# A fixed, interleaved instruction order and DMA transposes in a fused attention and GLU kernel on one Trainium2 core

## The chip, the cores and the metric

The kernel runs on one core of a Trainium2 chip. The metric is the device time of one execution in microseconds (us). The kernel before takes 261.02 us (median of 16 runs, 260.28 to 262.19).

PE is TensorE, the matrix engine, and PEld are its weight loads. DVE is VectorE, ACT is ScalarE, POOL is GpSimd and SP is the engine whose queue issues nearly all of the DMAs. The "span" is the time from the first to the last event of the profiled execution; the measured time is about 1.8 us longer.

## The reference

```python
xn = layernorm(x)                       # x: 2048 x 512, bf16
# branch A: linear attention, 32 heads of 16
q, k, v = split(xn @ wqkv)
phi(t)  = concat(softmax(t @ w_phi), softmax(-(t @ w_phi)))     # per head
kv, z   = phi(k)^T v, sum(phi(k))
o       = (phi(q) kv) / (phi(q) z + 1e-6)
# branch B: bilinear GLU, F = 1792
h       = (xn @ w_gate) * (xn @ w_up)
out     = x + o @ wo + h @ w_down
```

The sequence is 16 tiles of 128 tokens, in 4 groups. Both branches need xn with the features on the partitions, so xn is transposed; so are o and, for the fold of w_phi into wk and wq, the two weights.

## The kernel before

Each token tile passes through `a1_tile` (keys and values). The groups of four tiles then pass through the query stage, and the GLU and the output sum (`fin`) stand last in the source. A scheduler orders the instructions of every engine; it starts GLU matmuls early where it finds room.

```python
def ln_group(ng):                       # layer norm of 4 tiles, then transposes on PE
    ...
    for c in range(DC):
        tp = ps_tr.tile([P, TT], BF16, name="tp")
        for ni in range(GT):
            nc.tensor.transpose(out=tp[:, ni * P:(ni + 1) * P],
                                in_=xn_tiles[ni][:, c * P:(c + 1) * P], identity=ident[:])
        nc.scalar.copy(out=xnT[:, c, ng * TT:(ng + 1) * TT], in_=tp[:])

def a1_tile(n):
    pk = xnT tile @ W1k                               # PE, 4 matmuls of 512 columns
    e  = exp(pk), exp(-pk)                            # ACT
    vp = xnT tile @ wv ; vt = copy(vp)                # PE, ACT
    sums, rs, phik = reduce, reciprocal, e * rs       # DVE
    kv += phik^T vt                                   # PE, 8 matmuls of 129 columns

# query stage, per tile: nd on PE, five DVE steps, o_tok on POOL, then
otp = ps_pq.tile([P, DC, P], BF16, name="pq")
for c in range(DC):
    nc.tensor.transpose(out=otp[:, c, :], in_=o_tok[:, c * P:(c + 1) * P], identity=ident[:])
nc.scalar.copy(out=oT[:, :, n * P:(n + 1) * P], in_=otp[:])

# GLU, per block f: g = xnT @ wg (4 matmuls), u = xnT @ wu (4), g_sb = copy(g) on ACT, hT = u * g_sb on DVE
# fin, per tile: 14 matmuls hT @ wd and 4 matmuls oT @ wo
```

(The lines of `a1_tile` and the comments are shortened.)

The softmax here doesn't subtract the row's maximum and nothing guards it: scores larger than these inputs give would overflow.

## Time and profile before

| | before |
|---|---|
| time, span | 261.02 us, 258.8 us |
| PE busy | 92% of the span |
| DVE, ACT busy | 57%, 40% |
| first matmul starts, last ends | 5.4 us, 255.1 us |
| PE work, counted at issue pace | 226.5 us |

From the page of the kernel before: busy time by engine, three of the lines of 40 slices (tenths busy, and for PEclk the granted clock in tenths), and the head of the chain of work that ended last.

```profile
PE 239.3 (92%) x1376; PEld 115.5 (45%) x1376; DVE 148.1 (57%) x263; ACT 104.0 (40%) x209; POOL 22.2 (9%) x41
...
PE   0599999999999999999989999989999999999994
...
DVE  4286999999939972880983785487211211233221
...
PEclk9999999999999999999999999999999999999999
...
PE 67%; DVE 17%; POOL 5%; DMA 3%; ACT 2%; issue 2%; SPq 1%; POOLq 1%; DVEq 0%; ACTq 0%
```

PE looks full from the third slice on, yet only 67% of the chain is PE. Matmuls overlap in the records: one is on record for 0.38 us, but the next starts after 0.216 us. A gap of up to 0.16 us between two starts therefore does not show as idle, and a longer one shows 0.16 us too short. The busy share of 92% is therefore no good measure of the gaps here. The remedy used is to count work at issue pace: the number of matmuls of each kind, times the distance between starts where they follow each other without a wait.

That distance can be read where many stand together. From the timeline of the kernel before (start, length, then engine, line, operation and count; in brackets the idle time before it and what ended it), first at the beginning, then in the query stage:

```profile
11.40 0.63 PE L152 MATMUL tp<-ident,xn 128*128 128x128 bf16 x4
11.82 0.63 PE L188 MATMUL vp<-wv,xnT 128*128 128x512 bf16 x1
12.25 0.63 PE L279 MATMUL g<-xnT,wg 128*128 128x512 bf16 x1
...
106.78 0.40 PE L269 MATMUL pq<-ident,o_tok 128*128 128x128 bf16 x4 [0.52 <-POOL o_tok L264]
107.02 0.81 PE L279 MATMUL g<-xnT,wg 128*128 128x512 bf16 x3
107.67 1.03 PE L284 MATMUL u<-xnT,wu 128*128 128x512 bf16 x4
108.53 0.59 PE L279 MATMUL g<-xnT,wg 128*128 128x512 bf16 x2
108.96 0.66 PE L247 MATMUL nd<-KVZ,E 128*128 128x144 bf16 x8
```

At 107.67 four matmuls take 0.86 us (108.53 less 107.67). Around 12 us a single matmul takes 0.43 us, twice the steady 0.216; from 14.31 us on the pace is the steady one. That the clock is still low around 12 us is read from this pace alone: the PEclk row reads 9 there as well. Until 8.96 us PE waits for the layer norm of the four tiles; then the work comes in single matmuls, one chunk of xnT at a time. By 16.0 us only 12 full-width matmuls have started. At 106.78 PE has waited 0.52 us for o_tok. The waits list of the kernel before (engine and line, waited for, total us, times, longest) has these:

```profile
PEld L269 <- POOL o_tok L264: 13.1, 16, 1.0
PEld L152 <- DVE xn L146: 10.7, 10, 5.4
PE tp L152 <- DVE xn L146: 8.1, 4, 5.4
...
PE pq L269 <- POOL o_tok L264: 5.4, 12, 0.5
```

In sum PE issues 226.5 us of work in the 249.7 us between its first and last matmul: some 23 us are gaps (time lost to the half pace at the start is counted among them).

### The profile page before, as it was taken

The page shows a single profiled execution, that of the slowest core. Times are in us where ns is not written, and L with a number is a line of the kernel's source. Part 1 is how long each engine was busy: PE and PEld are TensorE (multiplying, and loading weights), DVE is VectorE, ACT ScalarE, POOL GpSimd, SP SyncE. Part 2 cuts the span into 40 slices and gives each one's busy share as a digit, 9 for nine tenths or more (in the row PEclk, how much of TensorE's full clock was granted, in tenths as well). Part 3 has the DMA queues.
Part 4 walks back from the last instruction along what each step waited for, and adds up shares of the span by engine and source line. Part 5 has one row for each costly group of instructions (what it writes and reads, how often), then busy time and mean ns, then how long its engine had stood idle before and what let it go on. Part 6 is the DMA issues. An engine that isn't in the chain of part 4 may idle for free.

```text
span 258.8 us, 3516 instructions
## 1 busy us (share of the span) xinstructions
PE 239.3 (92%) x1376; PEld 115.5 (45%) x1376; DVE 148.1 (57%) x263; ACT 104.0 (40%) x209; POOL 22.2 (9%) x41
## 2 busy tenths in 40 slices
PE   0599999999999999999989999989999999999994
PEld 0255444555454554444444454444444444444441
DVE  4286999999939972880983785487211211233221
ACT  3459745776367457248336445624000000013000
POOL 5200000000000000131131113033000000000000
PEclk9999999999999999999999999999999999999999
DMA  6999600000000000000000000000001101100001
GB/s 188 364 389 349 214 1 4 0 0 3 0 0 0 3 0 0 3 1 0 3 1 0 0 3 0 0 3 0 11 31 43 35 26 41 37 27 0 20 20 41
DMA packets 11007, 12.02 MB, mean 46 GB/s; under 512 B 1008, under 2 KB 9968, under 8 KB 10992
## 3 DMA queue, kind: packets, MB, share of 16 engines
q1 hardware_dynamic: 10992, 11.81, 13.8%
q8 instruction: 10, 0.16, 0.3%
q14 instruction: 5, 0.04, 0.1%
HBM read 9.72 MB, written 2.10 MB: 46 GB/s over the span
## 4 chain that ended last, share of the span: by engine, by line
PE 67%; DVE 17%; POOL 5%; DMA 3%; ACT 2%; issue 2%; SPq 1%; POOLq 1%; DVEq 0%; ACTq 0%
PE fin L295 19%; PE u L284 14%; PE g L279 11%; PE pq L236 6%; POOL o_tok L264 5%; PE fin L298 5%; DVE sums L194 5%; DVE hT L290 4%; DVE phik L198 3%; DMA wg<-in_B_w_gate_dram 3%; PE vp L188 3%; PE pk L181 2%; PE pq L269 2%; PE tp L152 2%; PE kv L203 2%
## 5 line engine op out<-in xcount | busy, mean ns | idle before, releaser
L289 ACT CAST g_sb<-g 128x512 bf16<-128x512 f32 x56 | 32.9, 587 | 86.2 <-PE g L279 84.6
L279 PE MATMUL g<-xnT,wg 128*128 128x512 bf16 x224 | 63.5, 381 | 0.2
L284 PE MATMUL u<-xnT,wu 128*128 128x512 bf16 x224 | 62.0, 381 | 0.3 <-DVE hT L290 0.2
L290 DVE TENSOR_TENSOR hT<-u,g_sb 128x512 bf16<-128x512 f32 x56 | 38.4, 687 | 41.6 <-PE u L284 40.7
L295 PE MATMUL fin<-wd,hT 128*128 128x512 bf16 x224 | 51.0, 379 | 0.0
L301 DVE TENSOR_TENSOR o_sb<-fin,xall 128x512 bf16<-128x512 f32 x16 | 11.1, 692 | 51.0 <-PE fin L298 51.0
L295 PEld LDWEIGHTS <-hT 128*128 128x128 bf16 x224 | 21.9, 98 | 26.4
L284 PEld LDWEIGHTS <-wu 128*128 128x128 bf16 x224 | 21.0, 98 | 23.0 <-issue 3.7
L264 POOL TENSOR_TENSOR o_tok<-sm,rden 128x512 bf16<-128x512 f32 x16 | 16.9, 1056 | 155.2 <-PE u L284 134.0
L279 PEld LDWEIGHTS <-wg 128*128 128x128 bf16 x224 | 21.1, 98 | 19.1 <-DMA wg<-in_B_w_gate_dram 0.7
L194 DVE TENSOR_REDUCE sums<-e 128x64 f32<-128x1024 f32 x16 | 19.2, 1201 | 0.4 <-ACT e L185 0.4
L198 DVE TENSOR_TENSOR phik<-e,rs 128x1024 bf16<-128x1024 f32 x16 | 19.4, 1211 | 0.0
L188 PE MATMUL vp<-wv,xnT 128*128 128x512 bf16 x64 | 18.9, 389 | 0.0
L181 PE MATMUL pk<-W1k,xnT 128*128 128x512 bf16 x64 | 17.8, 377 | 0.5
L152 PE MATMUL tp<-ident,xn 128*128 128x128 bf16 x64 | 9.1, 240 | 8.8 <-DVE xn L146 8.1
L298 PE MATMUL fin<-wo,oT 128*128 128x512 bf16 x64 | 16.4, 379 | 0.0
L270 ACT COPY oT<-pq 128x512 bf16<-128x512 bf16 x16 | 9.4, 585 | 17.0 <-PE pq L269 16.5
L236 PE MATMUL pq<-xnT,W1q 128*128 128x512 bf16 x64 | 15.6, 378 | 0.0
L141 DVE BATCH_NORM_STATS2 stats<-xall 128x6 f32<-128x512 bf16 x16 | 10.5, 675 | 7.6 <-DMA xall<-in_A_x_dram 7.6
L184 ACT ACTIVATE e<-pk 128x512 f32<-128x512 f32 x16 | 9.6, 599 | 10.8 <-DVE phik L198 5.7
L152 PEld LDWEIGHTS <-xn 128*128 128x128 bf16 x64 | 5.7, 106 | 15.1 <-DVE xn L146 10.7
L154 ACT COPY xnT<-tp 128x512 bf16<-128x512 bf16 x16 | 9.4, 590 | 6.3 <-PE tp L152 6.1
(48 smaller groups left out, 204.8 us busy)
## 6 DMA issues: line engine op xcount, KB each, us to landing
out_dram<-o_sb SPq DMA_DIRECT2D x16, 128.0 KB, 1.7
wd<-in_B_w_down_dram SPq DMA_DIRECT2D x1, 1792.0 KB, 13.6
xall<-in_A_x_dram SPq DMA_DIRECT2D x3, 512.0 KB, 12.3
wg<-in_B_w_gate_dram SPq DMA_DIRECT2D x1, 1280.0 KB, 11.2
wu<-in_B_w_up_dram SPq DMA_DIRECT2D x1, 1280.0 KB, 12.6
wqk<-in_A_wqkv_dram SPq DMA_DIRECT2D x2, 512.0 KB, 7.8
wv<-in_A_wqkv_dram SPq DMA_DIRECT2D x1, 512.0 KB, 6.7
wg<-in_B_w_gate_dram SPq DMA_DIRECT2D x1, 512.0 KB, 7.6
```

Of the source, the lines that this page charges most:

```text
L181: nc.tensor.matmul(pk[:], lhsT=xnT[:, j, n * P:(n + 1) * P], rhs=W1k[:, j, :], start=(j == 0), stop=(j == DC - 1))
L188: nc.tensor.matmul(vp[:], lhsT=xnT[:, j, n * P:(n + 1) * P], rhs=wv[:, j, :], start=(j == 0), stop=(j == DC - 1))
L194: nc.vector.tensor_reduce(out=sums[:], in_=ev, axis=AX.X, op=ALU.add)
L198: nc.vector.tensor_tensor(out=phik[:].rearrange("p s (h f) -> p (s h) f", f=DH), in0=ev, in1=rs[:].to_broadcast((P, 2 * H, DH)), op=ALU.mult)
L236: nc.tensor.matmul(pq[:], lhsT=W1q[:, j, cq * P:(cq + 1) * P], rhs=xnT[:, j, T * TT:(T + 1) * TT], start=(j == 0), stop=(j == DC - 1))
L264: nc.gpsimd.tensor_tensor(out=o_tok[:].rearrange("p (a h d) -> p a h d", a=2, d=DH), in0=sm[:, :, :, 0:DH], in1=rden[:].to_broadcast((P, 2 ...
L279: nc.tensor.matmul(gps[:], lhsT=wg[:, c, f * P:(f + 1) * P], rhs=xnT[:, c, T * TT:(T + 1) * TT], start=(c == 0), stop=(c == DC - 1))
L284: nc.tensor.matmul(ups[:], lhsT=wu[:, c, f * P:(f + 1) * P], rhs=xnT[:, c, T * TT:(T + 1) * TT], start=(c == 0), stop=(c == DC - 1))
L289: nc.scalar.copy(out=g_sb[:], in_=gps[:])
L290: nc.vector.tensor_tensor(out=hT[:, f, :], in0=ups[:], in1=g_sb[:], op=ALU.mult)
L295: nc.tensor.matmul(fin[:], lhsT=hT[:, f, t4 * P:(t4 + 1) * P], rhs=wd[:, f, :], start=(f == 0), stop=False)
L298: nc.tensor.matmul(fin[:], lhsT=oT[:, c, n * P:(n + 1) * P], rhs=wo[:, c, :], start=False, stop=(c == DC - 1))
```

## The change

There are two ideas in one change. The first: the order of every engine is written by hand (`manual_schedule`). A GLU block (1.73 us of PE) stands after each step whose result has to come back from ACT or DVE, the kv matmuls of a tile come one pass late, and `fin` is interleaved with `nd`. The second: 144 of the 160 transposes leave PE. xn (tiles 4 to 15) and o_tok are stored to DRAM and read back by a transposing DMA; wk and wq are loaded by a transposing DMA. Twelve dummy matmuls on zeros are added at the start, meant to raise the clock before the real ones (without them the time was 1.6 us longer: e5 below).

```diff
+    ctx.enter_context(tc.manual_schedule())
-    oT = xpool.tile([P, DC, S], BF16, name="oT")
+    oT = xnT
+    nc.sync.dma_start_transpose(out=wkT[:], in_=A_wqkv[:, D:2 * D])
...
+    wps = ps_gu.tile([P, TT], F32, name="gu")
+    for i in range(10):
+        nc.tensor.matmul(wps[:], lhsT=warm[:, 0:P], rhs=warm[:], start=True, stop=True)
...
-            for c in range(DC):                       # transposes of xn on PE, copies on ACT
-                tp = ps_tr.tile([P, TT], BF16, name="tp")
-                ...
+            nc.sync.dma_start(out=xds[ng][(ni - 1) * P:(ni + 1) * P, :]..., in_=xns[ng][:, ni - 1:ni + 1, :])
+            if ni == GT - 1:
+                nc.sync.dma_start_transpose(out=xnT[:, :, ng * TT:(ng + 1) * TT], in_=xds[ng][:])
...
-        for n in range(NT):
-            if n % GT == 0 and n > 0:
-                ln_group(n // GT)
-            a1_tile(n)
+        for n in range(NT):                           # G() is one GLU block
+            RED(n)
+            G()
+            if n >= GT: VV(n)
+            if n > 0: KV(n - 1)
+            LNr, LNx, TRst for the tiles of a later group
+            RCP(n); PHI(n)
+            G()
+            LNs for the tiles of a later group
+            PK(n + 1); EX(n + 1)
+            G()
...
-                otp = ps_pq.tile([P, DC, P], BF16, name="pq")       # transposes of o_tok on PE
-                ...
+            nc.sync.dma_start(out=ods[T][t4 * P:(t4 + 1) * P, :], in_=o_tok[:])
+            ...
+                nc.sync.dma_start_transpose(out=oT[:, :, T * TT:(T + 1) * TT], in_=ods[T][:])
...
+        for n in range(NT):
+            ND(n)
+            Pq(T + 1, t4, ps_pq, "pq")
+            Fin(fin_next) if n > GT else G()
```

(Shortened in places; the bodies are those of the kernel before. The GLU, `fin` and the first transposes share one PSUM pool of three banks.)

## The prediction

> **What bounds it now.** 261.35 us, span 258.8. The page gives TensorE (PE) 92% busy, VectorE 57%, ScalarE 40%; the chain of waits is 67% PE. Busy hides gaps, because matmul records overlap, so I count issue pace from the timeline: a 512-column matmul every 0.216 us (fin x14 in 3.02), nd x8 0.50, kv x8 0.47, a 128-column transpose or fold 0.056. The groups list 928 512-column matmuls, 128 nd, 128 kv, 160 transposes (64 of xn, 32 of wqk, 64 of o_tok) and 32 fold matmuls: 200.2 + 8.0 + 7.5 + 9.0 + 1.8 = 226.5 us. PE runs from 5.4 to 255.2, 249.8 us, so about 23 us are gaps. About 6 of them lie before 16 us: until 14 us matmuls are 0.43 us apart (cold clock[...]) and wait for layer-norm tiles (waits list: weight loads on xn 10.7 us, matmuls 8.1 us). The rest are short waits on VectorE, ScalarE and o_tok, scattered by the automatic schedule. The tail after the last matmul is 3.7 us.
>
> **What the change does.** A hand-fixed order on every engine: GLU blocks (1.73 us of PE each) lie between the attention steps so that PE has work during each VectorE/ScalarE latency; fin is interleaved with nd. 144 of 160 transposes move to the DMA (xn of groups 1 to 3, wk, wq, o_tok): minus 8.1 us of PE and about 36 PSUM copies. Adds 12 dummy matmuls that warm the clock while PE waits anyway, about 28 DMA issues, and some 7 MB of DRAM traffic on a queue idle after 32 us.
>
> **Cost on the critical path.** PE work left: 226.5 - 8.1 = 218.4. About 6.1 us of it (16 transposes, fold, four vp, one pk) precede the steady loop, which I expect to start at 14 us: first xn at 5, transposed wk near 8 to 9. Then 212.3 us of PE. Per tile PE needs 7.5 us with vp, 6.5 without; VectorE (sums 1.20, phik 1.21, rs 0.54, three hT 2.06, layer norm 1.25) needs 6.3, so PE stays the limit except in tiles 0 to 2, where two layer norms fall in one tile: about 2 us lost. Change of stage and bank waits: 1.5 us. Tail 3.3 us. Span 233, plus 2.2 us by which the time exceeds the span: **235 us**, range **230 to 244**. Chances: faster by over 2% 0.96, within 2% 0.03, slower 0.01.
>
> **Signs.** Right: PE pace 0.86 per four matmuls nearly unbroken from 14 us to the end; gaps under 6 us after the loop starts; cold matmuls only before 6 us; 1,232 real matmuls. Wrong: pk or vp of tiles 4, 8, 12, or fin of tiles 0 and 12, waiting for the DMA to xnT.
>
> **What would break it.** No transposing DMA is in this trace. [...] The slack from layer norm to first use is about 8.5 us, less 2 for the store, and at the end about 5 us; if a transpose takes 8 us, each of four places loses 2 to 3 us (about 245). A late wk delays the start one for one. [...]

14 + 212.3 + 2 + 1.5 + 3.3 make the span of 233, and with 2.2 the 235 us. "Cold" here means the pace of 0.43 us a matmul; that the dummies warm the clock had no measurement yet (e5 below gives one).

## The result, and the profile after

| | before | after |
|---|---|---|
| time (median) | 261.02 us (16 runs) | 230.34 us (8 runs, 230.03 to 231.11) |
| span | 258.8 us | 228.6 us |
| PE busy | 92% | 98% |
| matmul records | 1,376 | 1,262 |
| first real matmul starts, last ends | 5.4, 255.1 us | 5.53, 225.85 us |

The ratio of the times is 0.8823 (95% interval 0.8805 to 0.8841). Ratios here are the mean time of one kernel's fast runs over that of the other's of the same rounds, so not quite the ratio of the medians.

The same parts of the page of the changed kernel:

```profile
PE 224.2 (98%) x1262; PEld 111.8 (49%) x1262; DVE 150.8 (66%) x261; ACT 86.1 (38%) x177; POOL 22.4 (10%) x42
...
PE   7999999999999999999999999999999999999995
...
DVE  4769998877977786676557447996555556762121
...
PEclk9999999999999999999999999999999999999999
...
PE 98%; ACT 0%; DVE 0%; issue 0%
```

The chain is now PE and nothing else. The timeline of PE in the changed kernel, at the start of the loop and around the only wait for another engine that its waits list has for a PE matmul of the loop or later:

```profile
12.77 1.03 PE L143 MATMUL gu<-xnT,wg 128*128 128x512 bf16 x4
13.63 1.03 PE L149 MATMUL gu<-xnT,wu 128*128 128x512 bf16 x4
14.49 1.03 PE L143 MATMUL gu<-xnT,wg 128*128 128x512 bf16 x4
...
132.14 1.02 PE L180 MATMUL vp<-xnT,W1q 128*128 128x512 bf16 x4 [0.31 <-ACT E L183]
```

Each group of four starts 0.86 us after the one before it. That is the pace of the steady parts of the kernel before, now held from 12.8 us to the end with one gap of 0.31 us.

The 30.2 us of span can be booked by subtraction. PE work falls from 226.5 to 218.4 us, 8.1 us less. The gaps between first real and last matmul fall from 23.2 us (249.7 less 226.5) to 1.9 us (220.3 less 218.4), 21.3 us less. The time after the last matmul falls from 3.7 to 2.75 us, and the first real matmul starts 0.1 us later. The sum is 30.2. Of the gaps, about 5 us went at the start: by 16.0 us the changed kernel has started about 35 full-width matmuls, against 12 (23 x 0.216 us).

The DMA issues of the changed kernel, from its page (median us from issue to landing last):

```profile
xd<-xn SPq DMA_DIRECT2D x6, 256.0 KB, 2.1
...
xnT<-od SPq DMA_TRANSPOSE x5, 4.3
xnT<-xd SPq DMA_TRANSPOSE x3, 4.4
wT<-in_A_wqkv_dram SPq DMA_TRANSPOSE x2, 5.4
```

A store and a transpose of one group take about 6.5 us, and no matmul waits for them.

### The profile page after: what moved, and what is told of

It is laid out like the page before. It is cut to its first block, busy times and chain, and to the rows that moved or that the text cites. A ratio compares the mean times of both kernels' runs of the same rounds, so it can differ in the third digit from the quotient of the medians.

```text
span 228.6 us, 3315 instructions
## 1 busy us (share of the span) xinstructions
PE 224.2 (98%) x1262; PEld 111.8 (49%) x1262; DVE 150.8 (66%) x261; ACT 86.1 (38%) x177; POOL 22.4 (10%) x42
## 3 DMA queue, kind: packets, MB, share of 16 engines
q1 hardware_dynamic: 33040, 18.88, 29.4%
## 4 chain that ended last, share of the span: by engine, by line
PE 98%; ACT 0%; DVE 0%; issue 0%
PE gu L162 21%; PE gu L149 21%; PE gu L143 21%; PE gu L167 6%; PE pk L254 6%; PE vp L267 5%; PE pq L180 5%; PE nd L393 4%; PE kv L294 3%; PE gu L130 2%; PE vp L180 1%; PE pk L267 1%; PE gu L219 1%; PE pk L241 0%; PE kv L254 0%; PE pk L180 0%
## 5 line engine op out<-in xcount | busy, mean ns | idle before, releaser
L149 PE MATMUL gu<-xnT,wu 128*128 128x512 bf16 x224 | 57.5, 379 | 0.0
L143 PE MATMUL gu<-xnT,wg 128*128 128x512 bf16 x224 | 57.5, 379 | 0.0
L151 DVE TENSOR_TENSOR hT<-gu,g_sb 128x512 bf16<-128x512 f32 x56 | 38.4, 686 | 21.6 <-PE gu L149 21.6
L162 PE MATMUL gu<-wd,hT 128*128 128x512 bf16 (+2 forms) x238 | 51.2, 366 | 0.0
L146 ACT CAST g_sb<-gu 128x512 bf16<-128x512 f32 x56 | 32.9, 588 | 26.5 <-PE gu L143 26.5
L169 DVE TENSOR_TENSOR o_sb<-gu,xall 128x512 bf16<-128x512 f32 (+2 forms) x17 | 11.2, 660 | 35.0 <-PE gu L167 35.0
L143 PEld LDWEIGHTS <-wg 128*128 128x128 bf16 x224 | 21.3, 98 | 22.9
L276 DVE TENSOR_REDUCE sums<-e 128x64 f32<-128x1024 f32 x16 | 19.4, 1210 | 3.1 <-ACT e L262 3.1
L167 PE MATMUL gu<-wo,xnT 128*128 128x512 bf16 (+2 forms) x68 | 16.6, 366 | 0.0
L269 ACT CAST vt<-vp 128x512 bf16<-128x512 f32 x14 | 8.2, 587 | 14.3 <-PE vp L267 14.3
L406 DVE TENSOR_TENSOR sm<-nd,tmp 128x544 f32<-128x544 f32 x16 | 11.6, 725 | 1.5
L201 DVE BATCH_NORM_STATS2 stats<-xall 128x6 f32<-128x512 bf16 x16 | 10.9, 678 | 1.9 <-DMA xall<-in_A_x_dram 1.9
L403 DVE TENSOR_TENSOR tmp<-nd,rho 128x544 f32<-128x544 f32 x16 | 11.6, 725 | 0.5
```

Source lines behind the costliest of these rows:

```text
L143: nc.tensor.matmul(gps[:], lhsT=wg[:, c, f * P:(f + 1) * P], rhs=xnT[:, c, T * TT:(T + 1) * TT], start=(c == 0), stop=(c == DC - 1))
L146: nc.scalar.copy(out=g_sb[:], in_=gps[:])
L149: nc.tensor.matmul(ups[:], lhsT=wu[:, c, f * P:(f + 1) * P], rhs=xnT[:, c, T * TT:(T + 1) * TT], start=(c == 0), stop=(c == DC - 1))
L151: nc.vector.tensor_tensor(out=hT[T][:, f, :], in0=ups[:], in1=g_sb[:], op=ALU.mult)
L162: nc.tensor.matmul(fin[:], lhsT=hT[T][:, f, t4 * P:(t4 + 1) * P], rhs=wd[:, f, sl], start=(f == 0), stop=False)
L167: nc.tensor.matmul(fin[:], lhsT=oT[:, c, n * P:(n + 1) * P], rhs=wo[:, c, sl], start=False, stop=(c == DC - 1))
```

## The experiments

Two theories were put against each other. Theory O says that the order closes the gaps and the DMA transposes are worth just the PE time that they take off. Theory T says that the gaps came from the transposes and the chains around them, so that moving them to the DMA is what closed the gaps.

### The two ideas apart: four corners

e3 keeps the hand order and puts the transposes of xn (tiles 4 to 15) and of o_tok back on PE:

```diff
-                if m % 2 == 1:
-                    TRst(m)
...
+            for m in xm:
+                TRpe(m)                               # after the second GLU block
...
-            nc.sync.dma_start(out=ods[T][...], in_=o_tok[:])   # and the transposing DMAs
+        def OT(n):                                    # one pass later
+            otp = ps_gu.tile([P, DC, P], BF16, name="gu")
+            for c in range(DC):
+                nc.tensor.transpose(out=otp[:, c, :], in_=ods[n][:, c * P:(c + 1) * P], identity=ident[:])
+            nc.scalar.copy(out=oT[:, :, n * P:(n + 1) * P], in_=otp[:])
```

> The changed kernel, hand order kept, but the 48 transposes of xn tiles 4 to 15 and the 64 of o_tok are put back on TensorE (112 x 0.056 = 6.3 us of PE work), with their ScalarE copies. Theory O (the order closes the gaps; the DMA transposes are worth only the PE time they take off): 230.3 + 6.3 = 236.6 us, 235.5 to 239, PE still without gaps. Rival T (the gaps of the kernel before came from the transposes and the chains through PSUM copies around them; taking them off PE is what closed the gaps): 245 us or more, with PE waiting at the transposes and the copies.

e4 keeps the automatic order of the kernel before and moves the same 112 transposes to the DMA:

```diff
+            if ng > 0:
+                xd = dpool.tile([TT, D], BF16, name=f"xd{ng}")
+                for ni in range(GT):
+                    nc.sync.dma_start(out=xd[ni * P:(ni + 1) * P, :], in_=xn_tiles[ni][:])
+                nc.sync.dma_start_transpose(out=xnT[:, :, ng * TT:(ng + 1) * TT], in_=xd[:])
+                return
...
-                (transposes of o_tok on PE and the copy)
+                nc.sync.dma_start(out=od[t4 * P:(t4 + 1) * P, :], in_=o_tok[:])
+            nc.sync.dma_start_transpose(out=oT[:, :, T * TT:(T + 1) * TT], in_=od[:])
```

> The kernel before, automatic order, but the same 112 transposes (xn tiles 4 to 15, o_tok) go through DRAM and a transposing DMA. Theory O: 261 less 6.3 of PE work, so 253 to 257 us, gaps of some 20 us remain. Rival T: gaps close as well, 242 us or less. A third outcome, that the automatic order handles the DMA latency badly and the time does not fall at all (260 or more), would say the two parts need each other.

Both gave the right result. Medians in us:

| | transposes on PE | transposes by DMA | difference |
|---|---|---|---|
| automatic order | 261.04 (before) | 249.75 (e4; ratio 0.9557) | 11.3 |
| hand order | 237.41 (e3; ratio 0.9088) | 230.34 (after; ratio 0.8823) | 7.1 |
| difference | 23.6 | 19.4 | |

The hand-order row also has what else the change brings: the start with its dummies, the DMA transposes of wk and wq, and the PSUM layout.

Theory O holds for most of it. With transposes on PE, the hand order and what comes with it are worth 23.6 us. No run has the order alone. Of the 23.6 us, 1.8 are the PE work of the transposes of wk and wq (32 at 0.056), the dummies are worth about 1.6 (e5 below) and the third PSUM bank up to 4.8 (e6 below). If these simply add up, an estimate, some 15 us are left for the order. With the hand order the 112 transposes cost 7.1 us, close to their 6.3 us of PE work, and PE has no new wait: its only one for another engine in the loop and after is again the 0.31 us at the change of stages. But e4 fell below the 253 to 257 us that theory O expected, and theory T has a part. In the automatic order the transposes cost 5.0 us more than their 6.3 us of work. The likely place is the wait of PE for o_tok, 5.4 us in the kernel before, which is absent from the waits list of e4; between 120 and 180 us the idle time of PE falls from 4.1 us in the kernel before to 0.7 us in e4. No run took this wait away alone. In the hand order a transpose comes a whole pass after its o_tok, so there is no such wait to save. The two parts therefore overlap, and their single gains (23.6 and 11.3) add up to more than the 30.7 of both.

### Is it the written order, or the fixing of it?

e1 takes out the one line that fixes the order of the changed kernel:

```diff
-    ctx.enter_context(tc.manual_schedule())
+    pass
```

> The changed kernel with the one line that fixes the order taken out, so the scheduler may reorder; the source order still guides it. Theory O: gaps come back, 236 to 250 us, at most half of the gain lost since the source is already interleaved. Rival (the written interleaving, not the fixing of it, is enough): within 1% of 230.3 us.

It took 237.72 us (ratio 0.9088), 7.4 more than the changed kernel. Its timeline of PE shows where:

```profile
15.44 1.03 PE L143 MATMUL gu<-xnT,wg 128*128 128x512 bf16 x4
20.52 1.86 PE L149 MATMUL gu<-xnT,wu 128*128 128x512 bf16 x4 [4.05 <-ACT g_sb L146]
```

and of DVE in the same stretch:

```profile
17.64 1.29 DVE L201 BATCH_NORM_STATS2 stats<-xall 128x6 f32<-128x512 bf16 x2 [5.66 <-DMA xall<-in_A_x_dram]
...
20.16 1.20 DVE L276 TENSOR_REDUCE sums<-e 128x64 f32<-128x1024 f32 x1
```

The scheduler put the layer norm of tile 4 and on ahead of the sums of tile 0 on DVE. DVE sat 5.66 us waiting for a load of x, and the sums came after it. ACT waited for the results (up to 4.4 us, says its waits list) and PE for ACT. PE lost 4.05 us and came back at half pace (four matmuls in 1.7 us; the 16 from 20.52 us on took 6.3 us where the steady pace is 3.5; the mean granted clock of the run is 0.986). The first kv matmuls start 8.0 us later than in the changed kernel (28.54 against 20.54 us), and the whole span is 7.6 us longer. Of the 8.0 us, 0.9 were lost before the loop (which starts at 13.71 instead of 12.77 us) and 7.1 in this one place: from there on the automatic order held the pace. The interleaved source is worth more than the fixing of it: e1 is 12.0 us faster than e4, which has the old source (with the start, the transposes of wk and wq and the PSUM layout in that sum), while the fixing is worth 7.4 us and prevents one bad placement.

e2 gives the kernel before its own source order, stage after stage, fixed:

```diff
+    ctx.enter_context(tc.manual_schedule())
```

> The kernel before with its own written order fixed (stage after stage, no GLU blocks between the attention steps). Theory O says that it is the interleaving that counts: without fill PE waits in the attention stages for VectorE (16 tiles of about 3.7 us VectorE work, over 2.2 us PE) and in the num/den stage for o_tok: 285 to 330 us. Rival (taking the scheduler away is a gain in itself): below 261 us.

It took 460.25 us (one run, so its state is unknown; the profile has a mean clock of 0.825). Fixing an order is no gain in itself. The size was far from the 285 to 330 us expected. In the attention stage a tile takes 6.75 us (from the kv matmuls at 107.70 to those at 114.45 us) for about 2.2 us of PE work:

```profile
107.70 0.70 PE L204 MATMUL kv<-vt,phik 128*128 128x129 bf16 x8 [2.74 <-DVE phik L199]
108.19 1.91 PE L182 MATMUL pk<-W1k,xnT 128*128 128x512 bf16 x4
109.90 1.85 PE L189 MATMUL vp<-wv,xnT 128*128 128x512 bf16 x4
114.45 0.64 PE L204 MATMUL kv<-vt,phik 128*128 128x129 bf16 x8 [2.70 <-DVE phik L199]
```

My estimate left out that the matmuls between such waits would run at half pace: after the wait of 2.74 us pk takes 1.71 us for four matmuls, twice 0.86, and the mean granted clock of the run is 0.825, against 1.0 in the kernel before. Here a gap was paid twice, once as a wait and again in the matmuls after it. That is about 1.7 us of each such tile, not the whole excess: the chain over ACT and DVE was longer than estimated too, and in the query stage PE waits 61.8 us for o_tok. How the rest divides was not worked out.

### Distance between producer and consumer

e8 moves the kv matmuls of a tile from the next pass into its own, behind the second GLU block. The work is the same.

```diff
-            if n > 0:
-                KV(n - 1)
...
             PHI(n)
             G()
+            KV(n)
```

> The changed kernel with the kv matmuls of a tile in the tile's own pass, after the second GLU block, instead of one pass later. Same work. Theory O (it is the distance between producer and consumer that closes the gaps): PE reaches kv 4.3 us into the pass and phik ends 4.5 to 6.05 us into it, so about 1.1 us are lost in each of tiles 0 to 3, 1.7 in 4 to 10, 0.3 in 11 to 15: 18 us in sum, 240 to 252 us, with PE waiting for phik by name. Rival (the GLU blocks between are fill enough whatever the distance): below 233 us.

It took 248.35 us (ratio 0.9517), 18.0 more than the changed kernel and as expected. PE waits for phik by name; two of its eleven waits over 0.8 us, from the timeline:

```profile
50.77 0.64 PE L294 MATMUL kv<-vt,phik 128*128 128x129 bf16 x8 [1.55 <-DVE phik L287]
59.87 0.64 PE L294 MATMUL kv<-vt,phik 128*128 128x129 bf16 x8 [1.55 <-DVE phik L287]
```

Fill alone is not enough. Between pk and its kv there are now three GLU blocks and vp, 6.0 us of PE (3 x 1.73 + 0.86). With the wait of 1.55 us that makes 7.6 us, which is about how long the way over ACT and DVE takes, where other work stands in the queue too. The eleven waits come to 15.9 us on record. The passes of tiles 4 to 10 grew by 1.72 us each (from 7.38 to 9.10), 0.17 us more than the wait shows, because the record of the last matmul outlasts its issue (0.38 against 0.216 us); eleven times 0.17 brings the sum near 18 us. One pass more of distance makes it free.

### Why the early tiles did not lose 2 us

The prediction charged 2 us to the early tiles, where DVE has more work than PE. The result had no wait there. e6 takes one of the three PSUM banks away:

```diff
-    ps_gu = ctx.enter_context(tc.tile_pool(name="ps_gu", bufs=3, space=PSUM))
+    ps_gu = ctx.enter_context(tc.tile_pool(name="ps_gu", bufs=2, space=PSUM))
```

> The changed kernel with two PSUM banks instead of three for the GLU, fin and transposes. The trace of the changed kernel has VectorE without a pause from 13.2 to 38.7 us, its hT ending up to 2.3 us after the last matmul of its input, and PE still not waiting. Theory B (the third bank lets VectorE run behind, which is why the 2 us that I charged to tiles 0 to 2 did not come): PE now waits for hT and g_sb in every tile, most in the first four, 235 to 243 us. Rival (VectorE is simply fast enough and the banks have nothing to do with it): below 232 us.

It took 235.18 us (ratio 0.901), 4.8 more. The passes of tiles 4 to 10 lengthen from 7.38 to 7.63 us, and by the kv matmuls of the last tile (133.75 against 129.47 us) 4.3 us have been lost, so most of it in the attention loop. By name PE waits for hT only twice (0.28 and 0.43 us); the rest is in pauses too short to show. The first four tiles lost the most for one tile, 1.7 us together (their kv matmuls start at 20.94, 27.98, 34.70 and 42.67 us against 20.54, 27.05, 33.56 and 40.94), but not most of the sum, as I had expected. That they are near the 2 us of the prediction proves nothing: the later tiles, where DVE has time to spare, lose 0.25 us each as well. In the changed kernel DVE does fall behind in this stretch; its timeline has no pause between 14.8 and 38.7 us (the one before, of 0.32 us, the expectation overlooked):

```profile
19.90 1.21 DVE L276 TENSOR_REDUCE sums<-e 128x64 f32<-128x1024 f32 x1
...
26.79 1.21 DVE L276 TENSOR_REDUCE sums<-e 128x64 f32<-128x1024 f32 x1
...
29.74 1.22 DVE L287 TENSOR_TENSOR phik<-e,rs 128x1024 bf16<-128x1024 f32 x1
30.88 0.68 DVE L151 TENSOR_TENSOR hT<-gu,g_sb 128x512 bf16<-128x512 f32 x1
31.48 0.68 DVE L201 BATCH_NORM_STATS2 stats<-xall 128x6 f32<-128x512 bf16 x1
```

This hT ends at 31.56 us; the last matmul of its input ended at about 29.4 (the u block that starts at 28.38 and lasts 1.03). With three banks the block that needs the same bank starts at 31.83 us, 0.27 us later; with two it would have been due at 30.97. So the third bank is what lets DVE run behind.

The trace also shows how little DVE is over its time. From one sums to the next, its passes take 6.68 us (from 13.22 us on, with that pause in it), 6.89 and 6.10 us, against 6.51 of PE. That is at most 0.55 us too much in two passes, most of it won back in the third. The prediction had put the two passes 2 us over PE.

### The slack of the transposes

e7 issues each 512 KB transpose into xnT twice, the second after the first has landed:

```diff
-                nc.sync.dma_start_transpose(out=xnT[...], in_=xds[ng][:])
+                for _ in range(2):
+                    nc.sync.dma_start_transpose(out=xnT[...], in_=xds[ng][:])
```

(The same for the transposes of o_tok of groups 1 to 3.)

> The changed kernel with each 512 KB transpose into xnT issued twice, the second after the first has landed (same data, so the result stays right); TensorE has the same work. A transpose pair then takes 8.6 to 9.4 us instead of 4.3 to 4.7. My reading of the trace gives a slack from landing to first use of about 1.5, 1.1, 1.1 us for tiles 4, 8, 12 and 0.6 us for fin of tile 12; so PE waits 2.8 to 3.8 us at each of the four places, 12 to 15 us in sum: 242 to 246 us. The prediction had a slack of about 2.5 us at three places and 1 at the end: 8 us in sum, 238. If the slack is larger than both: below 234 us.

It took 249.88 us (ratio 0.9571), 19.5 more, above all that was expected. A pair lands 8.4 to 9.3 us after it was issued. The timeline of PE has six waits for these DMAs, 14.6 us in sum. The four longest, the last two with the matmuls that followed:

```profile
39.90 1.04 PE L255 MATMUL pk<-W1k,xnT 128*128 128x512 bf16 x4 [2.24 <-DMA xnT<-xd]
...
70.70 1.04 PE L255 MATMUL pk<-W1k,xnT 128*128 128x512 bf16 x4 [2.85 <-DMA xnT<-xd]
...
103.35 1.89 PE L255 MATMUL pk<-W1k,xnT 128*128 128x512 bf16 x4 [2.98 <-DMA xnT<-xd]
105.03 1.80 PE L143 MATMUL gu<-xnT,wg 128*128 128x512 bf16 x4
...
230.35 1.89 PE L167 MATMUL gu<-wo,xnT 128*128 128x512 bf16 x4 [3.70 <-DMA xnT<-od]
232.03 5.30 PE L162 MATMUL gu<-wd,hT 128*128 128x512 bf16 x14
```

The waits at tiles 4, 8 and 12 (2.2 to 3.0 us) and at fin of tile 12 (3.7 us) are about as read from the slack, the time from landing to the first matmul that needs the data. In the trace of the changed kernel it is 1.7, 1.0 and 1.6 us for tiles 4, 8 and 12, and 4.1, 2.5 and 0.7 us for fin of tiles 4, 8 and 12. Two things were not expected. fin of tiles 4 and 8 waited too (0.6 and 2.2 us). And after the waits of 2.98 and 3.70 us the matmuls ran at half pace, which cost 1.6 us (8 matmuls in 3.3 us) and 2.9 us (18 in 6.8 us); the mean granted clock was 0.84 from 99 to 110 us and 0.77 from 225 to 240 us. After the waits of 2.24 and 2.85 us they ran at full pace (0.87 us for four). The 14.6 of the waits and these two are 19.1 us of the 20.1 by which the span grew; six waits shown 0.17 us too short (as in e8) are the other 1.0. So the slack of the changed kernel is 1.0 to 1.7 us at the three tiles of the loop and 0.7 us at the end: its DMA transposes are free, but only just.

### The dummies, and the start

e5 leaves out the 12 dummy matmuls.

> The changed kernel without its 12 dummy matmuls. Theory (the clock counts: real matmuls from 6.9 us on would run at half pace, 0.43 us apart[...]): 4 us at half pace cost 2 us, so 231.5 to 234 us. Rival (the start is bound by the data and the layer norm, not by the clock): within 0.5 us of 230.3.

It took 231.93 us (ratio 0.8892), 1.6 more. (e5 to e8 ran on another chip, where the kernel before took 260.5 us, 0.5 less; by the ratios the difference is 1.8.) Its PE timeline shows the half pace until about 10.9 us:

```profile
6.64 1.89 PE L267 MATMUL vp<-wv,xnT 128*128 128x512 bf16 x4
8.32 1.91 PE L267 MATMUL pk<-wv,xnT 128*128 128x512 bf16 x4
...
11.81 1.04 PE L267 MATMUL vp<-wv,xnT 128*128 128x512 bf16 x4
```

The two groups take 3.4 us (6.64 to 10.03) instead of 1.7. Full pace came some 5.5 us after the first matmul at 5.36, with pauses in between. The mean granted clock of the run is given as 1.0, so the half pace is read from the starts of the matmuls alone.

Three more runs were made on one chip, two of them attempts to beat the changed kernel. e0 is the changed kernel again. e10 has nine dummies before the first transposes in place of ten (`range(10)` to `range(9)`). e9 asks for the transposed wk before x and wv, moves these to the other queue and folds before the first vp:

```diff
-    dma_x(0, 1); dma_x(1, 2); dma_cols(wv, ..., nc.sync)
-    (wphi and x tiles 2, 3 on the ACT queue; then wk by a transposing DMA)
+    (x tiles 0 and 1, wv, x tiles 2, 3 on the ACT queue)
+    nc.sync.dma_start(out=wphi[:], ...)
+    nc.sync.dma_start_transpose(out=wkT[:], in_=A_wqkv[:, D:2 * D])
...
-        (two dummies)
+        foldj(wkT, W1k, 0, kvb[0]) ... foldj(wkT, W1k, 3, ...)
```

> The changed kernel again, unchanged, as the baseline for the two runs beside it on the same chip: 230.3 us, 229.8 to 231.

> An attempt to beat the changed kernel at its start: the transposed wk is asked for first, x and wv come on the other queue, the fold (0.9 us of PE) is done before the first vp, in the time in which PE runs dummies and waits for the copy of xnT, and one dummy fewer. If wk lands by about 6 us and wv is not later than 7: 229.5 us, about 0.8 less. If wv comes later through the shared engines, or the four copies of W1k delay xnT of tiles 1 to 3: 230.5 to 232.5. Both within 1%.

> The changed kernel with nine dummy matmuls first instead of ten: in its trace the first real transpose waits 0.3 us for the last dummy (xn at 5.2 us, transpose at 5.53). If the clock still rises as early: 0.2 us less. If the clock rises later: up to 1 us more.

e0 took 230.55 us (ratio 0.8844) and e10 230.18 us (ratio 0.8827). The intervals (0.8817 to 0.8871 and 0.8795 to 0.8859) overlap, so e10 is not shown to be faster. Its four runs (230.05 to 230.31) do lie below the four of e0 (230.42 to 230.71), but by no more than executions of one kernel differ: the eight of the changed kernel span 230.03 to 231.11. e9 took 236.9 us (ratio 0.9088). PE stood for the very transpose that was asked for first:

```profile
11.69 1.46 PE L241 MATMUL kv<-BD,wT 128*128 128x128 bf16 x12 [5.26 <-DMA wT<-in_A_wqkv_dram]
```

It was issued at 1.33 us and landed at 11.64. In the changed kernel it is issued at 2.19 and lands at 8.08, and the fold starts at 8.66 us without a wait. After the wait the matmuls ran at half pace (four of vp in 1.71 us, from 13.37 to 15.08; the mean granted clock of the run is 0.986, against 0.999 in e0), which adds to the loss. The one known difference is that more plain loads of both queues were in flight beside it, and these were late as well (wv took 8.9 us against 4.5, x of tiles 2 and 3 9.2 against 3.6); the order in which the DMA engines served them was not looked into, so the mechanism stays open.

## Why the prediction was right

The median is 230.34 us; 235 was predicted, with a range of 230 to 244. The main mechanism was right (PE work at full pace, with few gaps), and the sum was 4.7 us too high, so that the result lies near the lower end of the range. The measured PE work from the loop on is what the trace has between 12.77 and 225.85 us less the one wait. Term by term:

| term | predicted | measured |
|---|---|---|
| start of the steady loop | 14 us | 12.77 us |
| from there to the last matmul: PE work | 212.3 us | 212.8 us |
| DVE limit in the first tiles | 2 us | 0 |
| change of stage, bank waits | 1.5 us | 0.3 us |
| tail | 3.3 us | 2.75 us |
| time over span | 2.2 us | 1.7 us |

- PE work and pace. "PE work left: 218.4" with a pace of 0.86 us per four matmuls was right: 1,262 records less the 12 dummies are 1,250, which is the 1,232 predicted and 18 more because the last fin is split in two.
- "First xn at 5, transposed wk near 8 to 9" was right: the first transpose ran at 5.53 us and the fold at 8.66. The loop started 1.2 us sooner than I put it, because the order left no pause between these steps.
- "VectorE needs 6.3, so PE stays the limit except in tiles 0 to 2 ... about 2 us lost" is the term that was mis-sized most. DVE does fall behind in these tiles, but I booked its lag as PE time, and the lag was too large: two passes of DVE took 6.68 and 6.89 us against 6.51 of PE, at most 0.55 us over and not 2. With three banks PE needs an hT only three bank uses later, and DVE catches up before it costs anything. e6 showed that the third bank is needed for this; how much of its 1.7 us in the first four tiles is DVE's excess was not separated.
- "Change of stage and bank waits: 1.5 us" was too high; one wait of 0.31 us was left.
- A DMA transpose of 512 KB into xnT took 4.2 to 4.7 us; the prediction's own estimate of it rested on no trace. "Slack about 8.5 us, less 2 for the store", less that estimate too, left about 2.5 us and was too large; the trace puts it at 1.0 to 1.7 us, and e7 bears that out. That it sufficed all the same was partly luck. That "each of four places loses 2 to 3 us (about 245)" if a transpose takes 8 us was too low: with 8.4 us and more, e7 took 249.88 us, as the matmuls after the two longest waits (2.98 and 3.70 us) ran at half pace and two more places waited.
- The signs named as right are in the profile, but for one detail: the eight transposes from 5.53 to 6.39 us still run at half pace, just past the 6 us named. Those named as wrong are not in it.

## What to carry to other kernels

Where one engine has nearly all the work, count its work at issue pace and call the rest of its time gaps, since its busy share can hide them (here 92% with 23 us of gaps). Here the gaps closed when other work lay between each producer and its consumer for longer than the whole way over the other engines takes (one pass later, not in the same pass: 18.0 us in e8) and with one buffer more (the third bank: 4.8 us in e6); so DVE could fall behind for two tiles (6.68 and 6.89 us a pass against 6.51 of PE) at no cost. Look at how thin the slack is before building on it: here a transpose twice as long turns 19.5 of the 30.7 us back, because there are six waits (14.6 us) and the matmuls after the two longest ran at half pace (4.5 us).

## What else the traces show

- The share of weight loads is 45% before and 49% after, though PE had 23 us of gaps before and 1.9 after: a load takes 98 ns and a 512-column matmul 216 ns. At issue pace it would be 51% (115.5 of 226.5 us, and 111.8 of 218.4). Held against that it says 88% and 96%, just what the issue pace says.
- The six DMA transposes of 512 KB into xnT took 4.2 to 4.7 us in the changed kernel, and the two of 256 KB 3.2 and 3.8. That is about 0.9 us for 256 KB more, so about half of the 4.2 to 4.7 us does not grow with the size (an estimate from these two sizes). wk took 10.3 us from issue to landing in e9, against 5.9 in the changed kernel.
- The issue of a transpose took 1.2 to 2.2 us on the SP timeline of the changed kernel for those into xnT, and 3.8 us for wk at the start (a store of o_tok mostly 0.33).
